# Hash sums in half as many matmuls, late causal masks on VectorE and 64-bit weights scaled in place, in a fused attention kernel

## The chip, the cores and the metric

The kernel runs on one NeuronCore of one Trainium2 chip, and no other core takes part. The metric is the time of one execution of the whole program on the device, in microseconds (us). A core has five engines that run side by side, each through its own list of instructions in order: TensorE (PE in the profile, with its weight loads as PEld), VectorE (DVE), ScalarE (ACT), GpSimd (POOL) and SyncE (SP), which here only starts DMAs. PSUM is the memory that TensorE writes into; SBUF is the working memory. GpSimd has work on SBUF tiles only.

## The reference, cut to what matters

Three layers follow each other, on B = 2 sequences of S = 768 rows and 8 heads of 64 columns. The first is attention between rows with the same hash of 6 bits, the second a causal attention of 4 experts with a choice of 2, the third a feed-forward layer with a gate.

```python
def _attn_ref(q, k, v, proj):                      # q, k, v: 2 x 8 x 768 x 64; proj: 64 x 6
    q_bits = (np.einsum('bhsd,dk->bhsk', q, proj) > 0).astype(np.int64)
    k_bits = (np.einsum('bhsd,dk->bhsk', k, proj) > 0).astype(np.int64)
    powers = 2 ** np.arange(n_bits)
    q_bucket = np.sum(q_bits * powers, axis=-1)
    k_bucket = np.sum(k_bits * powers, axis=-1)
    mask = q_bucket[:, :, :, None] == k_bucket[:, :, None, :]
    scores = np.where(mask, scale * np.matmul(q, k.transpose(0, 1, 3, 2)), -1000000000.0)
    attn = softmax(scores)
    return np.matmul(attn, v)
...
def _moe_ref(x, w_gate, wq, wk, wv, wo):           # x: 2 x 768 x 512
    ...
    for e in range(E):                             # E = 4 experts, heads of 64 columns
        q, k, v = x @ wq[e], x @ wk[e], x @ wv[e]
        causal = np.triu(np.ones((S, S), dtype=bool), 1)
        scores = np.where(causal, -1000000000.0, scale * (q @ k.transpose(0, 2, 1)))
        ye = softmax(scores) @ v @ wo[e]
        out += (the weight of e where e is among the two highest) * ye
    return out
...
def _moe2_ref(x, mu_k, mu_r, w_k, w_v, w_r):       # w_k, w_v, w_r arrive as 64-bit floats
    x_prev = (x moved down by one row)
    xk, xr = mu_k * x + (1.0 - mu_k) * x_prev, mu_r * x + (1.0 - mu_r) * x_prev
    k = np.maximum(xk @ w_k, 0.0)
    return 1.0 / (1.0 + np.exp(-(xr @ w_r))) * (k * k @ w_v)
```

`softmax` and the words in brackets stand for lines that are left out.

## The kernel before

The rows are cut into 12 tiles of 128 (`NU`), tiles 0 to 5 of the first sequence and 6 to 11 of the second. For each tile `i` four groups of steps are recorded: the query (`query_steps`), the hash attention (`lsh_steps`, one score per head, then one product with the values per head), the expert attention (`moe_steps`) and the feed-forward layer (`mix_steps`). Keys come in groups of four heads (`key_steps(b, g)`, four groups in all), weights in `weight_steps`. Almost every operand is kept as a high and a low 16-bit part, so that a product takes three matmuls.

Four things of it matter here.

**The hash.** A query tile is turned by TensorE into `x2`, a key group into `y2`, and `hash_signs` multiplies each turned block of 128 rows with the projection, which stands in `prhl` as a high and a low part of 6 columns each. The two products are added in PSUM by accumulation, so a block takes two matmuls of 6 columns: 16 matmuls for a query tile (8 heads), 48 for a key group (24 blocks). `mark` then compares the sums in `z` (in PSUM) with zero, twice, and writes a large number or zero into spare columns of `nbq` (queries) or `nbk` (keys); these are turned in their place into `x1` and `y1`, and so the score of two rows with different hashes falls far below. `naq` and `nak` are the tiles that hold the high and low parts of a query tile and of half a key group before they are turned.

**The causal mask.** `score(c)` of `moe_steps` handles a pair of experts: TensorE writes both scores (`se`) into PSUM, and then adds `causal`, a triangle of very large negative numbers, to the last 128 columns of each by one more matmul with the identity. The minimum over a row, the exponential and the split into high and low parts (`P_m`, `PHL_m`) follow on VectorE, ScalarE and GpSimd, then a transpose by DMA (`PT_m`). The scores of both attentions share two PSUM buffers (`ps_s`).

**The 64-bit weights.** `split_d` loads the two 32-bit words of each number (`raw`). GpSimd scales the upper words into a tile of their own (`mag`, `wm` in the profile), and VectorE puts the number together from `mag`, `raw` and an exponent that ScalarE made. There are 20 such blocks.

**The order.** Nothing is scheduled while the kernel is built: all operations are recorded, and `arrange` (line 184) puts them into the order of a packed table, `ORDER`; a second table, `HOMES`, gives each tile its buffer. `issue` (line 199) then sends them to the engines, which is why every instruction bears the number of one line, 201. An engine works through its own instructions in that order, whatever it waits for.

Of the kernel before, what the change touches and what calls it, by code (L numbers as in the profile page):

```python
# [17 lines left out]
OP = mybir.AluOpType  # L18
# [210 lines left out]
def tile_lsh_moe_mix(  # L229
# [98 lines left out]
    def turn(dst, src, nm, by_dma=False):  # L328

        if by_dma:  # L330
            nc.sync.dma_start_transpose(dst, src)
            return
        n = src.shape[1] // P
        hn = n // 2
        if n > 8:
            pt = [dps(f"tr_{nm}_{j}").bitcast(F16)[:, :hn * P] for j in range(2)]
        else:
            pt = dps(f"tr_{nm}").bitcast(F16)
            pt = [pt[:, j * hn * P:(j + 1) * hn * P] for j in range(2)]
# [42 lines left out]
    def split_d(src, dst, sc, nm):  # L382
# [3 lines left out]
        mag = sp.tile([P, n], F32, tag="b2", bufs=NB2, name=f"wm_{nm}")  # L386
# [3 lines left out]
        nc.gpsimd.tensor_scalar(mag, top.bitcast(F32), REBIAS, 1.0, op0=OP.mult, op1=OP.mult)  # L390
# [3 lines left out]
        nc.vector.scalar_tensor_tensor(u, mag.bitcast(U32), 3, u, op0=OP.logical_shift_left, op1=OP.bitwise_or)  # L394
# [49 lines left out]
    def key_steps(b, g):  # L444
# [11 lines left out]
        def half(j):  # L456
            if j == 0:
# [40 lines left out]
    def query_steps(i):  # L498
# [4 lines left out]
        def prep():  # L503
# [9 lines left out]
            turn(x2, na.rearrange("p h c -> p (h c)"), f"x2_{i}", i in QD)  # L513

        def hash_():
# [4 lines left out]
            turn(x1, nb.rearrange("p h c -> p (h c)"), f"x1_{i}", i in QD)  # L520
# [19 lines left out]
    def hi_engine():  # L540
        NS[0] += 1
        return "p" if (NS[0] - 1) % 8 < 2 else "a"
# [98 lines left out]
    def moe_steps(i, LAG):  # L641
# [67 lines left out]
        def score(c):  # L709
# [196 lines left out]
c-jq?gAyQ062MwB-LtlB+qP}nwr$(CZQHhO<Jo)n4XIQ@0Km`^+CwHN2&Eu12sp?B(LmuOwt}881NuV;=m)K#7ZifhkPUJ`VJHL9Atw}r;!pxgLUyPKl^_O`  # L906
hYFAjVnbXg2eAObLslpXWuXYn1cS;DAP&TXJdhhAK~;zXRUk4{gX+)>T0nlN1vMZl)P|Zc3uZ$Bh!1&T4xGY#kPs5XX>1JX;V+H|F<}6-fws^QIzeY>2fd*<
=Er)F2ogXlD1fQqJf6i8SRV>v3doAt@Em5xlu!}}!d$q3^WbkD1QDP*CW9nU2n%Bo971VeB20oVFa!p}P}mI(peu}o95@+rVp1rDrLhLqfx0jSE@E8Fjh8Vw
oWV<Y1+QUq7zVj;4@`x4m>kPvUMz}vFazv`wU7cE!cf`=DKS1K!0VU~YvO)Lg$H07^nvwI3!6Y%7!GBy8;pX4m<ZQFYD|N}DL<FRL(t9bmW=QVHiCojD_+G7
PyshWMQjSgC><uo23QXtVOl&4wQ&<9!6VQeDq$V$0V7~K{D$eVG9HCUloab@20R9lDH%RSAxBZ@IQ)(oF%!;*Wl#m{VpZ%5nK3FA;B+vGM$io$O;6C%2`GpE  # L910
U@;s?o8czj!hbOfE{ABe0HV`qc#11vAuNL1xDx)u#jpyV;d4~FgLiQ??2(r^hQ`tdY>16;9KFJcv<4<oW2}bbsR=g43G@+{z*6{x_wWHW!?W}U{=oa#9E}1!
#MjsYx6<D@7Pi0zh(SP~aT|QWH`oeWVjFCY5$FZ}iCdu{Z=>z7op!)EYL9JkC%naza1p*D(qH%v-(x%61?Q;)E}?H2hbGe{_>Mbh3dN<La0teurSvln$Dvr5
nTm2BybS&E3iQRJ6qAUGa526>-Q5U04a2Y>UWH?H4PsG8EaAt&7&rxm_&6=2GZ2xA^IVEgXQ2z0<f*iicF}dXNCR*=jfasq3I}309E9Dm2hPFRRD$PG0y+ot
sVA1=)zlSN&`O#{rMVZLhtYTs5>gp1%X=viC8ojH8!yofn1E|&BA%d|&<Rh{TI!6Ga2+k6eUzM%(KzhD<8cg*#iW#kZoz(<jJIJoU8Vz+f~Me9yaOHiA0EN~
# [90 lines left out]
```

## Time and profile before

| What | us |
|---|---|
| Median of 3 runs (lowest, highest) | 470.1 (467.38, 470.42) |
| The profiled execution, whole | 470.66 |
| Its span, from the first to the last instruction | 468.9 |
| TensorE busy in it | 428.9 |
| VectorE busy | 345.3 |
| ScalarE busy | 345.0 |
| GpSimd busy | 324.2 |
| DMA queue of SyncE, share of 16 DMA engines | 85.4% |

All rows of the profile come from the one profiled execution; its span and the whole time differ by what lies before the first and after the last instruction. An engine that is busy is not always an engine that is waited for: which one sets the pace differs between the first 140 us and the rest, so the profile has to be read by stretches of time. The granted clock of TensorE was 0.981 of full speed on average.

### The profile page before, as it was taken

To read this page: it belongs to the slowest core of one execution; us is meant where nothing else is said; L and a number is where in the kernel's file an instruction comes from. 1 tells how busy PE (TensorE), PEld (TensorE's weight loads), DVE (VectorE), ACT (ScalarE), POOL (GpSimd) and SP (SyncE) were. 2 spreads that over 40 slices of the span, in tenths; PEclk is the share of its full clock that TensorE was granted. 3 is DMA by queue.
4 is the path that set the end of the run, shared out by engine and by line. 5 is a ranking of instruction groups with operands and counts; after the bars stand their busy time and mean duration, and the time that the engine had idled before them with its cause. 6 is when DMAs were issued, how large, how long until landed. Compare 5 with 4: busy or idle time off the path is not lost.

```text
span 468.9 us, 15555 instructions
## 1 busy us (share of the span) xinstructions
PE 428.9 (91%) x6296; PEld 328.6 (70%) x6296; DVE 345.3 (74%) x970; ACT 345.0 (74%) x654; POOL 324.2 (69%) x321
## 2 busy tenths in 40 slices
PE   2965679899899999998999999999999999999996
PEld 1843467677777779787777778687668769867572
DVE  3999989989999779899695667955768644643421
ACT  4369889979999889777985977878777975543320
POOL 5579899879886977876989468857766945362000
PEclk9997889989999999999999999999999999999999
DMA  8978989899999999989999799978998894555101
GB/s 228 284 191 194 198 191 180 171 225 170 181 219 199 204 178 192 191 157 181 164 184 170 158 148 150 179 148 141 141 156 119 140 187 82 126 81 125 46 24 45
DMA packets 227160, 75.59 MB, mean 161 GB/s; under 512 B 218512, under 2 KB 222736, under 8 KB 227088
## 3 DMA queue, kind: packets, MB, share of 16 engines
q1 hardware_dynamic: 225584, 74.48, 85.4%
q8 instruction: 49, 0.80, 0.7%
q10 hardware_dynamic: 1504, 0.11, 0.2%
q14 instruction: 23, 0.19, 0.1%
HBM read 22.14 MB, written 3.15 MB: 54 GB/s over the span
## 4 chain that ended last, share of the span: by engine, by line
PE 61%; DVE 11%; POOL 10%; DMA 8%; issue 6%; ACT 4%; SPq 0%; POOLq 0%; DVEq 0%; ACTq 0%
PE v L201 12%; PE h L201 11%; PE x L201 7%; PE s L201 7%; POOL PHL L201 6%; PE r L201 5%; PE qk L201 5%; DVE P L201 3%; DMA PT<-PHL 3%; PE se L201 3%; PE y L201 3%; PE o L201 3%; PE tr_y L201 2%; PE vg L201 2%; DMA PT_m<-PHL_m 1%
## 5 line engine op out<-in xcount | busy, mean ns | idle before, releaser
L201 POOL TENSOR_TENSOR PHL<-P,PHL 128x768 f16<-128x768 f32 x96 | 159.7, 1672 | 36.1 <-ACT PHL L201 34.4
L201 DVE TENSOR_SCALAR_CACHE_REDUCE P<-s 128x768 f32<-128x768 f32 x96 | 91.0, 951 | 19.1 <-PE s L201 12.7
L201 ACT ACTIVATE P<-P,mx 128x768 f32<-128x768 f32 x96 | 89.1, 928 | 16.3 <-DVE mx L201 15.7
L201 PE MATMUL s<-y,x 128*128 128x384 f16 x384 | 80.7, 336 | 8.7 <-DVE P L201 6.1
L201 PE MATMUL h<-mk,WK 128*128 128x128 f16 x1152 | 72.6, 219 | 0.0
L201 PEld LDWEIGHTS <-WK 128*128 128x128 f16 x1152 | 67.0, 98 | 4.0
L201 PE MATMUL x<-v,PT 128*128 128x64 f16 x1728 | 64.3, 195 | 2.1 <-DVE v L201 2.0
L201 PEld LDWEIGHTS <-PT 128*128 128x128 f16 x1728 | 60.2, 99 | 6.8 <-issue 2.4
L201 ACT ACTIVATE PHL<-P 128x768 f16<-128x768 f32 x72 | 59.9, 839 | 4.9 <-DMA PT<-PHL 1.6
L201 PEld LDWEIGHTS <-x 128*128 128x128 f16 x576 | 40.8, 99 | 28.8 <-issue 10.1
L201 PE MATMUL v<-WV,k2h 128*128 128x512 f16 x192 | 57.1, 379 | 0.0
L201 POOL TENSOR_TENSOR PHL_m<-P_m,PHL_m 128x512 f16<-128x512 f32 (+2 forms) x24 | 34.3, 1429 | 18.6 <-ACT PHL_m L201 10.2
L201 PE MATMUL qk<-xT,WQK 128*128 128x128 f16 x576 | 35.8, 219 | 1.0 <-DVE xT L201 0.5
L201 PE MATMUL v<-WV,k2l 128*128 128x512 f16 x96 | 36.4, 379 | 0.0
L201 PEld LDWEIGHTS <-WQK 128*128 128x128 f16 x576 | 33.1, 98 | 2.6 <-DMA xT<-hl_x 0.9
L201 PE MATMUL r<-WR,mr 128*128 128x512 f16 x144 | 34.5, 379 | 0.0
L201 DVE SCALAR_TENSOR_TENSOR h<-h,t 128x512 f32<-128x512 f32 x24 | 16.6, 694 | 20.7 <-ACT t L201 20.7
L201 ACT ACTIVATE t<-h 128x512 f32<-128x512 f32 x24 | 14.2, 590 | 23.4 <-PE h L201 23.3
L201 DVE TENSOR_SCALAR_CACHE_REDUCE P_m<-se 128x512 f32<-128x512 f32 (+2 forms) x24 | 19.6, 818 | 13.4 <-PE se L201 3.8
L201 PEld LDWEIGHTS <-k2h 128*128 128x128 f16 x192 | 17.0, 98 | 13.2 <-issue 0.2
L201 POOL TENSOR_SCALAR PHL<-P 128x768 f16<-128x768 f32 x24 | 21.0, 876 | 7.5 <-ACT P L201 3.5
L201 ACT ACTIVATE P_m<-P_m,bias_m 128x512 f32<-128x512 f32 (+2 forms) x24 | 19.7, 821 | 7.8 <-DVE P_m L201 7.7
(143 smaller groups left out, 867.8 us busy)
## 6 DMA issues: line engine op xcount, KB each, us to landing
raw_k<-in_moe_w_k_dram SPq DMA_DIRECT2D x8, 512.0 KB, 4.5
raw_v<-in_moe_w_v_dram SPq DMA_DIRECT2D x8, 512.0 KB, 4.3
q<-in_q_dram SPq DMA_DIRECT2D x12, 256.0 KB, 5.3
k<-in_k_dram SPq DMA_DIRECT2D x8, 384.0 KB, 5.2
v<-in_v_dram SPq DMA_DIRECT2D x8, 384.0 KB, 4.7
out_dram<-e SPq DMA_DIRECT2D x12, 256.0 KB, 2.6
raw_r<-in_moe_w_r_dram SPq DMA_DIRECT2D x4, 512.0 KB, 4.5
PT<-PHL SPq DMA_TRANSPOSE x88, 4.3
```

What stands on the lines that cost most here:

```text
L201: getattr(getattr(self.nc, engine), method)(*[real(a) for a in args], **{k: real(a) for k, a in kw.items()})
```

## The change

Four things are changed in the code, and with them both tables.

- `hash_signs` multiplies each block once with all 12 columns of `prhl`. ScalarE copies the 6 low sums of each block from PSUM into a new SBUF tile `zs`, VectorE adds the 6 high sums to them, and `mark` reads `zs` in SBUF where it read `z` in PSUM. 384 hash matmuls become 192; 16 copies on ScalarE and 16 additions on VectorE are new (12 of 48 columns, 4 of 144).
- For tiles 6 to 11 (`MV`) the causal mask is added to the scores by VectorE, in PSUM: one instruction for both experts where a score has at most 512 columns (tiles 6 to 9), else one for each. 24 matmuls of 128 columns go; 16 VectorE instructions come (8 of 256 columns, 8 of 128).
- `split_d` scales the upper words where they are, in `raw`, and `mag` is gone: 20 GpSimd instructions write every second word of `raw` where they wrote a dense tile, and VectorE reads them there.
- `turn` can leave a copy to ScalarE (`engs`), but `KE` and `QE` are empty, so it never does; `HP` is the old rule under a name.

```diff
+KE, QE = {}, {}
+MV = (6, 7, 8, 9, 10, 11)
...
-        z = dps(f"z_{nm}", [P, n, NB])
+        z = dps(f"z_{nm}", [P, n, 2 * NB])
         for j in range(n):
-            for a in (1, 0):
-                nc.tensor.matmul(z[:, j], rows(j), prhl[:, a], start=(a == 1), stop=(a == 0))
-        return z
+            nc.tensor.matmul(z[:, j], rows(j), prhl.rearrange("p a b -> p (a b)"), start=True, stop=True)
+        zs = sp.tile([P, n, NB], F32, tag="b2", bufs=NB2, name=f"zs_{nm}")
+        nc.scalar.activation(zs, z[:, :, NB:], AF.Copy)
+        nc.vector.tensor_tensor(zs, z[:, :, :NB], zs, op=OP.add)
+        return zs
...
-        mag = sp.tile([P, n], F32, tag="b2", bufs=NB2, name=f"wm_{nm}")
         raw = sp.tile([P, n, 2], U32, tag="b4", bufs=NB4, name=f"raw_{nm}")
         LOADS.dma_start(raw.rearrange("p n a -> p (n a)"), src.bitcast(U32))
         top = raw[:, :, 1]
-        nc.gpsimd.tensor_scalar(mag, top.bitcast(F32), REBIAS, 1.0, op0=OP.mult, op1=OP.mult)
+        nc.gpsimd.tensor_scalar(top.bitcast(F32), top.bitcast(F32), REBIAS, 1.0, op0=OP.mult, op1=OP.mult)
...
-        nc.vector.scalar_tensor_tensor(u, mag.bitcast(U32), 3, u, op0=OP.logical_shift_left, op1=OP.bitwise_or)
+        nc.vector.scalar_tensor_tensor(u, top, 3, u, op0=OP.logical_shift_left, op1=OP.bitwise_or)
...
-                                         stop=(a == 2 and j < len(parts) - 1))
+                                         stop=(a == 2 and (i in MV or j < len(parts) - 1)))
             d0 = t0 * P - k0
-            for r in range(2):
-                o = Sv[r] if one else Sv[r][:, j]
-                nc.tensor.matmul(o[:, d0:d0 + P], ident, causal, start=False, stop=True)
+            if i in MV and one:
+                d = both[:, :, d0:d0 + P]
+                nc.vector.tensor_tensor(d, d, causal.unsqueeze(1).to_broadcast([P, 2, P]), op=OP.add)
+            else:
+                for r in range(2):
+                    o = Sv[r] if one else Sv[r][:, j]
+                    if i in MV:
+                        nc.vector.tensor_tensor(o[:, d0:d0 + P], o[:, d0:d0 + P], causal, op=OP.add)
+                    else:
+                        nc.tensor.matmul(o[:, d0:d0 + P], ident, causal, start=False, stop=True)
...
 ORDER = """
-c-jq?gAyQ062MwB-LtlB+qP}nwr$(CZQHhO<Jo)n4XIQ@0Km`^+CwHN2&Eu12sp?B(LmuOwt}881NuV;=m)K#7ZifhkPUJ`VJHL9Atw}r;!pxgLUyPKl^_O`
+c-jru^8*)F7l83|&b{ZHd%oGWv8-h+bGf!`W6QPdWo=o@HkP)yW!rAqeBb}!`Qh^r0JMZQ;2;|mgW^yEvO^9i2j!sxl!4Na2RcJc=mfFA!*`Gu%0gAh1(hK-
...
```

Both tables are new from end to end, and every instruction's number changes. The long run of work is the same: tiles follow each other as before, and most pieces keep their neighbours. Three places show what moved. The first is the start of SyncE's list, which issues the loads (`w32` weights of the expert layer, `q32` and `k32` queries and keys before the split). Before:

```order
L201 DMA w32_qk01_79<-in_moe_wq_dram 128x4x64
L201 DMA q32_0_81<-in_q_dram 128x8x64
L201 DMA k32_0_1_0_83<-in_k_dram 128x2x384
L201 DMA k32_0_1_1_85<-in_k_dram 128x2x384
L201 DMA k32_0_0_1_93<-in_k_dram 128x2x384
L201 DMA k32_0_0_0_95<-in_k_dram 128x2x384
```

Now, on SyncE at the start:

```order
L208 DMA q32_0_81<-in_q_dram 128x8x64
L208 DMA k32_0_1_0_83<-in_k_dram 128x2x384
L208 DMA k32_0_1_1_91<-in_k_dram 128x2x384
L208 DMA w32_qk01_115<-in_moe_wq_dram 128x4x64
L208 DMA k32_0_0_1_117<-in_k_dram 128x2x384
L208 DMA w32_qk01_115<-in_moe_wq_dram 128x4x64
L208 DMA w32_qk00_150<-in_moe_wq_dram 128x4x64
L208 DMA k32_0_0_0_152<-in_k_dram 128x2x384
```

The first query and the first two halves of a key group moved up by one place; the last half of a key group moved down by two.

The second place is the start of VectorE's list, up to the first copies of turned blocks (`tr`) out of PSUM. Before:

```order
L201 CAST prhl_89<-pr32_72 128x6
L201 TENSOR_TENSOR prhl_89<-pr32_72,prhl_89 128x6
L201 SCALAR_TENSOR_TENSOR naq_0_87<-q32_0_81,naq_0_87 128x8x64
L201 SCALAR_TENSOR_TENSOR nak_0_1_0_111<-k32_0_1_0_83,nak_0_1_0_111 128x12x64
L201 SCALAR_TENSOR_TENSOR nak_0_1_1_113<-k32_0_1_1_85,nak_0_1_1_113 128x12x64
L201 COPY x2_0_128<-tr_x2_0_115 128x512
```

Now, on VectorE at the start:

```order
L208 SCALAR_TENSOR_TENSOR nak_0_1_0_85<-k32_0_1_0_83,nak_0_1_0_85 128x12x64
L208 SCALAR_TENSOR_TENSOR naq_0_88<-q32_0_81,naq_0_88 128x8x64
L208 SCALAR_TENSOR_TENSOR nak_0_1_1_93<-k32_0_1_1_91,nak_0_1_1_93 128x12x64
L208 CAST prhl_122<-pr32_72 128x6
L208 COPY y2_0_1_124<-tr_y2_0_1_0_0_103 128x768
L208 COPY x2_0_126<-tr_x2_0_110 128x512
```

The two operations on the projection moved from the head of the list to behind the first three splits.

The third place is VectorE at a late score, that of the first pair of experts of tile 7 (`se_7_0`): the minimum over it (`P_m7_p0`, one instruction per expert) is what stood there before.

```order
L201 TENSOR_SCALAR P_m7_p0_6403,bias_m7_1_6404<-se_7_0_6376 128x256
L201 TENSOR_SCALAR mx_9_5966<-mx_9_5966 128x1
L201 TENSOR_SCALAR P_m7_p0_6403,bias_m7_0_6407<-se_7_0_6376 128x256
L201 SCALAR_TENSOR_TENSOR m32k_6_6343<-o_6_6118,muk_289,x2t_6_1402 128x128
L201 SCALAR_TENSOR_TENSOR m32r_6_6438<-o_6_6118,mur_77,x2t_6_1402 128x128 x2
```

Now, on VectorE at the same score:

```order
L208 TENSOR_TENSOR se_7_0_6210<-se_7_0_6210,consts_74 128x2x128
L208 SCALAR_TENSOR_TENSOR m32r_6_6061<-o_6_5942,mur_78,x2t_6_2244 128x128
L208 TENSOR_SCALAR P_m7_p0_6231,bias_m7_0_6232<-se_7_0_6210 128x256
L208 SCALAR_TENSOR_TENSOR m32k_6_6064<-o_6_5942,muk_318,x2t_6_2244 128x128 x2
L208 TENSOR_SCALAR P_m7_p0_6231,bias_m7_1_6241<-se_7_0_6210 128x256
```

The addition of the mask stands two places ahead of the first minimum, with a piece of the feed-forward layer (`m32r`) between them.

## Rows read from the trace of the kernel before

**Rows 1.** Busy time of each engine in three stretches, granted clock, DMA share.
```profile
core 0: us, PE busy (x) PEld busy (x) DVE busy (x) ACT busy (x) POOL busy (x), PEclk, DMA share, GB/s
...
20.00:68.00 48.00, 31.77 (x404) 23.30 (x402) 45.71 (x107) 39.02 (x70) 41.52 (x37) 0.86 0.84 198
68.00:140.00 72.00, 65.27 (x1061) 52.28 (x1059) 68.03 (x208) 66.80 (x142) 64.22 (x69) 0.97 0.97 193
140.00:440.00 300.00, 296.62 (x4515) 229.75 (x4514) 211.68 (x618) 227.91 (x428) 206.35 (x197) 1.00 0.91 155
```

**Rows 2.** TensorE's costliest wait from 140 us on: total us, times, longest.
```profile
PE y L201 <- DMA PT_m<-PHL_m: 1.7, 2, 1.4
```

**Rows 3.** The chain that ended last, its last piece on an engine: start, us, what.
```profile
465.09 0.69 DVE e L201
```

**Rows 4.** Instructions of TensorE in order of time (start, us, count), 188 to 201 us.
```profile
188.98 1.34 PE L201 MATMUL z_k<-prhl,y 128*128 128x6 f16 x48
190.18 0.69 PE L201 MATMUL x<-v,PT 128*128 128x64 f16 x18
190.70 0.60 PE L201 MATMUL v<-WV,k2h 128*128 128x512 f16 x2
...
200.49 0.29 PE L201 MATMUL se<-consts 128*128 128x128 bf16 x2
200.61 1.34 PE L201 MATMUL z_k<-prhl,y 128*128 128x6 f16 x48
```

**Rows 5.** The start in order of time: two DMA issues, ScalarE, GpSimd, VectorE.
```profile
1.22 0.50 SPq L201 DMA_DIRECT2D q<-in_q_dram  x1
1.77 2.61 SPq L201 DMA_DIRECT2D k<-in_k_dram  x4
...
6.82 0.84 ACT L201 ACTIVATE nak<-k 128x768 f16<-128x768 f32 x1 [0.43 <-DMA k<-in_k_dram]
6.98 0.62 POOL L201 MEMSET nbk<- 128x624 f16 x1
7.07 0.55 DVE L201 CAST prhl<-pr 128x6 f16<-128x6 f32 x1 [7.07 <-DMA pr<-in_proj_dram]
7.91 2.71 POOL L201 TENSOR_SCALAR nbk<-k 128x768 f16<-128x768 f32 x2 [0.32 <-DMA k<-in_k_dram]
8.35 3.07 DVE L201 SCALAR_TENSOR_TENSOR nak<-k,nak 128x768 f16<-128x768 f32 x2
13.41 0.94 DVE L201 SCALAR_TENSOR_TENSOR nak<-k,nak 128x768 f16<-128x768 f32 x1
```

**Rows 6.** Groups, shapes apart: count, busy us, mean ns, idle before and its releaser.
```profile
L201 DVE TENSOR_SCALAR nbk<-z_k 128x72 f16<-128x72 f32 x16 | 2.9, 223 | 0.6 <-PE z_k L201 0.6
L201 DVE TENSOR_TENSOR y<-y,rse 128x256 f32<-128x256 f32 x12 | 5.0, 419 | 1.1 <-PE y L201 1.0
L201 DVE SCALAR_TENSOR_TENSOR m32k<-o,muk,x2t 128x128 f32<-128x128 f32 x48 | 15.6, 344 | 0.6 <-POOL mr L201 0.4
L201 POOL TENSOR_SCALAR wm_k<-raw_k 128x512 f32<-128x512 f32 x8 | 6.0, 756 | 3.6 <-DMA raw_k<-in_moe_w_k_dram 3.5
L201 ACT ACT_TABLE_LOAD x16 | 20.5, 1283 | 3.4 <-issue 3.1
L201 DVE SCALAR_TENSOR_TENSOR naq<-q,naq 128x512 f16<-128x512 f32 x12 | 11.0, 920 | 0.0
```

**Rows 7.** Tiles z_q and naq: ns (shortest/median/longest), first and last start.
```profile
L201 DVE TENSOR_SCALAR nbq<-z_q x24: 192/200/211, 16.5 to 322.9; 128x48 f16<-128x48 f32 x24
L201 DVE SCALAR_TENSOR_TENSOR naq<-q,naq x12: 679/741/1522, 7.7 to 260.4; 128x512 f16<-128x512 f32 x12
```

**Rows 8.** All engines in order of time, 294 to 300 us, three instructions of it.
```profile
294.61 3.25 POOL L201 TENSOR_TENSOR PHL<-P,PHL 128x768 f16<-128x768 f32 x2 [0.73 <-ACT PHL L201]
296.33 2.08 DVE L201 TENSOR_TENSOR hl_x<-x,hl_x 128x512 f16<-128x512 f32 x1 [0.36 <-ACT hl_x L201]
...
299.21 0.82 PE L201 MATMUL s<-y,x 128*128 128x384 f16 x4 [1.00 <-DVE P_m_p L201]
```

More of the change, by code (lines that the diff above doesn't have):

```diff
@@ L37, with HP @@
 OKV = 61440.0
+def HP(n):
+    return n % 8 < 2
+KE, QE = {}, {}
+MV = (6, 7, 8, 9, 10, 11)
 QD, KD, XD, YD = (8, 9, 10, 11), (), (8, 9, 10, 11), (8, 9, 10, 11)
@@ L541, in hi_engine @@
         NS[0] += 1
-        return "p" if (NS[0] - 1) % 8 < 2 else "a"
+        return "p" if HP(NS[0] - 1) else "a"
     def softmax(Sv, n, scale, sm, bias, nm, masked=None, by_pe=None):
@@ L910 @@
[L910 to L914, printed above, removed]
@@ new lines @@
+D`OVSir?Tjup0*QXc$f-Xb((-?D!W{$HLeH{)T-}A6G*rSOp`g4-A6__yhKY+n5H^;TlMfYhgcp!aJA)KVu6R4r%cKe2+D-AvVHMG=}2RXu6BPQal<<7qKzU
+fj^)o&V`(q3)ewzTns;AEj$RBVIGX5zR(ZGQ!`u-UobvRp!qP7E}<u;=6D(NU=?hNQ7IZNfGJc4?_mO30tsmZB%-f)A0OaUx`IGgaVboq$s}|Qm5`cXbc#VS
+sW!gAN4N}H;Bt70kMR|*fR=b2x6%n}g*Wguw#NVP3H}P=H$Y-K4iE7r-oke1XcN4_h42(NLM)0+-?_Iq6UV{{c!t|(Gi-rHaFW_!du)r-s1v53t<V9tQ%Bqe
+o$(}0r&Dl>0v!UP=eUGE;5+<?QOIZvB&V{jyc>e=aR>cLhoKehq|>yND!66z8%1b14#kvI&Ygx-l!WF{U+jm!U>96Y|G>X+2GozhVR#mP!k@9C8-Rx>DaE04
+&>cr&4;+O@U_MoH{qZQQpsv^x2V!M+n5wvc=oloUJ(QZ#P#HG}SJHX73Zt<XR(0KQFa1krC@l@f?_D)_maf4CI6~tf9bJS4)EjHK>aGuFq)e2a&e0|Ki^k)1
@@ new lines @@
+xB(MzBHn}yw3>d!u{aLL;O}%9{-zn!-35OICSg=R8P`w`mzi!sR+@rGX*|rNRdkGY(POv+-_TU7=^}otTS$v2nqNyjT@;^%dbxG9&)<e=_&d&_Su`Dg!+rDz
+?Wegk&dtDCxSozvHu{z>P%XECW>a?R?Fv$DSI6a~TvUi!xJ$H~HqvD}K#OS(&c)d{4|7u<%1i%2VQT5dyL{BjEyTt62j-ypxQRAXep-ZAXbaVKMW~N6-{1Y>
+o<LuBp6a_2)X-g|gR}sj!ZWxF_n@_F;M%wXRL|Xqt5ljEz;l@3iqb>4MlWEZTZt=h8AkWlDTZ(4O41FA=^MKN?h(ZDvHeXN=9c3R?nf8T$MNxfTtD1Rb?sez
+`~bzMI8AbsT@zP|zN4mY6@G#x*w*d$AEBA+;O^3G>gVpzElS`=xX-W#zd#vUjb*96ti_S;E8L?8G|&Mq#d?$g+qp-S5C^&Y^pFzz%GA+4p=b1*UQlyaj$XoJ
+dP<$#D3=JU&>Q;A{pu3qOZtyqQF$um5BURrutOZ;I=j*C6?AcguPF)s?%vZ|O5{J#JNigps45-yN%1S8JLoG=C8|hWT{Rl&{_)l66OD1*+-vyPm-cVqh@auU
@@ new lines @@
+^WPIWa5d;H9P`e-gMi+#`%GE=Pwr>;jju_yDY>8G()pwQJvhwfJ(lr_{YhVoj{7<^-A!{T{3(CJr}T{3{W`qlXS!J~hZjuZ)B6nmvR9n#>QX9i7;zbWCO^lm
+#|>D>Z^Ym>qdIfq>QhrH>>E%N*My?F<`m5p@mG99`hl9!kF*J6;EGUObNZydtdH-K`OH3oS$uB41-D{!w+(mUX}=ryU}_)3#l&*Hyien|;|^>=Eh!4-@li1v
+#&myTbj<5_Vk~#Y58|sn7N+&N{57A?Kl6L>FO1^~`q(b6tKcj8zp<8&jd3t8#>2Bdzc1<=Q6*p5SMhcHbN|B6bqm})H{X@?`*1&g@2~s8T);P`V!o;`?uW}u
+oxtDvKionW&s}iU{9?Dro%84YFdo9|-A;D^hjId!&<*DlE~QKEwz`-8mA~Li`0D<(f8&?9ByNMN>;HC%-Ex=6rE)d=Hn-jFa4X#^x7xL#z^$mJZ%ZS1glu&C
++zPkf9dK*hF1ObG=|=J<x7(G_rLMNG=SQ(|gj>^1f6KR{Wo|Slb@hEG>P%gzD>d*x_=9e<+v4`Pb#AZw%azn4u7$ttTl@ADg`;u@>PRhp8$XfT`e;0v+xhnX
@@ new lines @@
+u>02mKk$wGA@`4K=zr&n{)UgvW4M){#K_&~s5|C5_~WjlpTWQKIBx7uxT*Z3f9LP`yM88*W#aKXjZeBJ{*;@;Z+%Rj%hS23|BWB|NB>XJ^Er3Mopo{ewEOCN
+P&41$zxN;f&vf3+<I;MC@A)Zw-!pge!l${jzv!;G`TW@5a+ll<chy~XH{D17$uHoAyokHgPxPOk#ZUZI?n%Aqsqf-%yWVt-m-0yILw%_qDfg#e=r+gZoBY{-
+@dIce4Wh2Tn}4NeI4<Ae#ry}~;<KF0&F1cYW$58ky9<1Y2h&Bq%*%KM_wlhf9uJ`<yqs4u$aVhATN&jBpW~nW&;C4*lDmA5`}%?YK0o9K{D>bjNes^5(z~bJ
+&-e6${1+bV@3{W{8OP^z?j^tCUA&v0^MCB*1@GY}97leYRXkea${2|!d-*S3&BJ_Jw~o`eUcR^YvYuJSN_@HIGP-R%#1Hkq_yPWJP9O<o9}o8lI3d60{rrYS
+ruyqHlT%s4BYhM}#B2F2Z{T;lku$rflEo$CBs@+=_@q2uHgO^evYAKu13cOv<Y@AhCrETj$?rL<`^IH+M>sJjXOkVgg=0ue`M|McJ0Im#oZY47V?4&E;E9rs
@@ L962 @@
+TE;kW42V8N!5i0O|L93mg2}yh)+<oc$@{9E`P>?p2eJ6hy`Dbjfw@ewNl>IX)`(aJfzag-jmMbe_Tc|T7DP{y#apZvG}_15K73#0He%<4$E$LlHNV4mtw<J)
+<{)uh1>@>c&zWN9{#fy@wC*li)NK<+(_5NM%z187yxor*p37-w8-4=K+#E~
 """
```

95 lines of the change are left out of this document (41 added, 54 removed).

## The prediction, made before the changed kernel ran

> **What bounds the kernel now.** The averages of the whole run say that TensorE is busiest, but they mix two kinds of stretch, so I began with the busy times by stretch [rows 1]. From 20 to 68 us VectorE is busy 45.71 of 48 us and TensorE only 31.77: there VectorE sets the pace, with GpSimd (41.52) and ScalarE (39.02) behind it. From 68 to 140 us four engines are near full, none alone at the limit (VectorE 68.03, ScalarE 66.80, TensorE 65.27 of 72). From 140 to 440 us TensorE is busy 296.62 of 300 us and VectorE only 211.68. The waits of TensorE behind 140 us bear it out: the costliest, for a DMA that brings the turned weights of the expert attention, is 1.7 us in all [rows 2]. The chain of what ended last closes with VectorE's last result at 465.09 us [rows 3], and this end is the same in both kernels. So a microsecond taken from TensorE behind 140 us is worth nearly a microsecond, and one added to VectorE there nothing; before 68 us it is the other way round. The change takes from TensorE and gives to VectorE in both. The sum is made against the profiled execution, 470.66 us, which lies 0.56 above the median of the runs.
>
> **TensorE behind 140 us.** In the row of time order 48 hash matmuls of 6 columns start at 188.98 and the next work at 190.18 [rows 4]: 1.20 us, 25 ns each. The product with 64 columns takes 29 ns (18 from 190.18 to 190.70), so the number of columns hardly shows, and I cost a matmul of 12 columns at 25 ns too. Key groups of the second batch: 2 x 24 fewer x 25 ns = 1.2 us. Queries 6 to 11: 6 x 8 x 25 ns = 1.2 us. A pair of mask matmuls takes 0.12 us (200.49 to 200.61) [rows 4], 12 pairs are gone: 1.4 us. Together 3.8 us. Queries 3 to 5, in the mixed stretch, are 3 x 8 x 25 ns = 0.6 us, of which I count half, since TensorE is one of four near the limit there. Sum **-4.1 us**. Were 12 columns to cost 29 ns, the 96 matmuls that are left behind 140 us would take back 0.4.
>
> **The start.** VectorE does nothing until the projection arrives at 7.07 us. Then a cast of 6 elements takes 0.55 us and ends at 7.62, just when GpSimd's fill of `nbk` (6.98 + 0.62) ends [rows 5]: it looks held back by it. Two `nak` beside GpSimd's work on `nbk` (7.91, 2.71 long) take 3.07 us, one alone at 13.41 takes 0.94 [rows 5]: some 0.6 us lost on each. Now the first `nak` heads VectorE's list. Its keys are issued one place earlier, 0.55 us (1.77 less 1.22), so ScalarE's half, ended at 7.66 before (6.82 + 0.84), may end at 7.11: VectorE starts when it did, but without the blocked cast, 0.5 us. If the two `nak` also go free, 1.7 us are won; if GpSimd holds the first one for one more fill of 0.62 instead, 0.5 is lost. I take **-1.0 us**, the cast and one of the two `nak`, with bounds of -1.7 and +0.5.
>
> **The additions to the hash sums, until 68 us.** VectorE adds two key groups (144 elements) and three queries (48). The trace has no such form; the nearest rows are a comparison of 72 elements at 223 ns and a tensor operation of 256 at 419 ns [rows 6], which puts 144 at 0.30 us, and the mark of 48 elements at 200 ns [rows 7]. 2 x 0.30 + 3 x 0.20 = 1.2 us; instructions in a row overlap somewhat, I take 0.9: **+0.9 us**. ScalarE copies the low sums ahead of them; its 9 idle us of 48 cover five copies, each surely shorter than the 0.84 us of a `nak` half [rows 5]. If not covered, they delay VectorE by at most the 1.5 us that five of 0.30 make.
>
> **The marks.** This is the term with the widest bounds. A mark now reads SBUF where it read PSUM. From PSUM it was never held: shortest 192, median 200, longest 211 ns over 24 [rows 7]. An operation of VectorE that reads SBUF alone can be: `naq` takes 679 ns at its shortest and 1522 at its longest [rows 7], 920 in the mean [rows 6], so it loses 0.24 us on average, with GpSimd busy for much of the time. And near 296 us one `hl_x` took 2.08 us beside GpSimd's `PHL`, after which TensorE stood still for 1.00 us [rows 8]. Until 68 us there are 14 marks, 8 of key halves and 6 of queries, in 7 pairs; the bounds are nothing and 14 x 0.6 (the loss of a `nak` above) = 8.4 us. I take one average loss for each pair, since a mark is far shorter than `naq` and can slip in between two of GpSimd's instructions: 7 x 0.24 = **+1.7 us**. The Trainium skill says in "SBUF — State Buffer", section "Who interferes with whom", that VectorE and GpSimd share a pair of SBUF ports as an exclusive lock, held for a whole instruction, that single-source operations between SBUF tiles in a two-port mode contend for it, and that with a source in PSUM they can't enter that mode. By that rule every mark is moved from the forms that never wait into those that may, and the sum would come out as in the second rival below; the row of `naq` agrees that waiting occurs, no row shows it of a mark.
>
> **68 to 140 us.** Three additions (0.6) and three pairs of marks (3 x 0.24 = 0.7) for queries 3 to 5, half of it on the path in a stretch where VectorE is busy 94%: **+0.7 us**.
>
> **Edits at nothing.** The late masks on VectorE: 8 of 256 elements by 0.42 and 8 of 128 by 0.34 [rows 6] are 6.1 us, hidden in the 88 us that VectorE is idle from 140 to 440 (300 less 211.68); without that cover 6.1, the third rival. The scaling in place: 20 operations of 756 ns [rows 6], which read every second word before and now write so as well; VectorE reads `raw` in such steps already. At 0; were the eight early ones to double, 6 us on GpSimd, which has 6.5 idle us from 20 to 68. Two more loads of ScalarE's tables, by the order, at 1.28 us [rows 6]: covered by 72 idle us behind 140. That the new order makes or removes waits otherwise, I can't price beyond the 1.7 of [rows 2].
>
> **The sum.** -4.1 - 1.0 + 0.9 + 1.7 + 0.7 = -1.8: 468.9 against the profiled 470.66, and **468.3 us** against the median.
>
> **Rivals.** First, the marks aren't held (a pair that slips in, as every mark from PSUM does) and the start gives its full 1.7: -1.8 - 2.4 - 0.7 = -4.9; with half the wait of 1.7 gone in the new order, 0.8, it is -5.7, **464.4 us**. For it: marks are short. Against it: GpSimd is busy 87% of the time there.
>
> Second, on the other side, every mark is held for 0.6 us: the 1.7 becomes 8.4 until 68 us, and the 0.7 of the mixed stretch becomes half of 0.6 + 6 x 0.6, 2.1; -4.1 - 1.0 + 0.9 + 8.4 + 2.1 = +6.3, **476.4 us**. It decides from 0.23 us a mark: with 17 marks that count (14 and half of 6), 17 x 0.23 = 3.9 is what the other terms (-4.1 - 1.0 + 0.9 + 0.3) win. For it: the `nak` at the start; against it: the median of `naq`, 741 ns, is only 62 above its shortest, so most go nearly free.
>
> Third, the mask on VectorE is a new wait: it stands between a score and its minimum, on one of the two PSUM buffers that all scores share, so the next score on TensorE can start only when VectorE got to both. If VectorE comes late each time, 6.1 us land on TensorE: -1.8 + 6.1 = +4.3, **474.4 us**. For it: TensorE did wait 1.00 us for a minimum [rows 8]; against it, it did so only there, in 300 us.
>
> Last, a matmul of 12 columns may cost twice one of 6, so that only the masks are saved: 1.4 instead of 4.1, and 471.0 us; I hold that as part of the forecast's own case, since 64 columns at 29 ns speak against it.
>
> **Chances.** The forecast's case, 466.5 to 471.0 us, has 0.42; the free marks 0.33; the held marks 0.15; the late mask 0.10. A measurement of this kernel can tell about 1% from no change, 465.4 and 474.8 us. Faster than that are some seven tenths of the first rival (0.23) and a little of the forecast's case (0.05): 0.28. Slower are three quarters of the held marks and half of the late masks: 0.17. The rest, 0.55, is the same. The range goes from 463.0, the first rival with all of the 1.7 us wait gone (463.5) and a little more, to 474.5, which takes in the late mask and leaves out the upper half of the held marks.
>
> **What would show it.** Right: 192 hash matmuls at 25 ns a piece; VectorE at work on `nak` by 7.2 us; the first 68 us of work shorter or longer by no more than 2 us; marks of `zs` with a median near 200 ns and some above 500; TensorE's waits behind 140 us still near 3 us. The second rival: marks over 500 ns throughout, and idle TensorE before 68 us that grows. The third: waits of TensorE's scores for VectorE's minimum or mask behind 140 us, several us in all. I would be wrong altogether if the granted clock, 0.86 of full speed from 20 to 68 us [rows 1] (the levels are 1.2 and 2.4 GHz), fell for longer because TensorE has less to do early, or if the new order made a wait that no row here shows.

## The result, and the profile after

The changed kernel takes 472.12 us (median of 16 runs, 470.72 to 474.25), the kernel before 467.44 us in the 16 runs now beside it (464.08 to 470.75): ratio 1.0106, 95% interval 1.0085 to 1.0128. It is slower by 4.7 us, where 1.8 us less was forecast, and its absolute time lies within the range only because the three runs of before that were shown (470.1) lay high. Its profiled execution has a span of 471.3 us.

The busy times by stretch, in the columns of [rows 1]:

```profile
20.00:68.00 48.00, 33.54 (x376) 23.43 (x377) 47.63 (x110) 40.36 (x75) 39.72 (x37) 0.83 0.84 189
68.00:140.00 72.00, 60.77 (x990) 48.66 (x987) 71.38 (x205) 63.64 (x136) 61.93 (x69) 0.98 0.93 193
140.00:440.00 300.00, 294.42 (x4392) 225.64 (x4390) 226.70 (x645) 233.52 (x442) 207.79 (x198) 1.00 0.89 154
```

VectorE is now busy almost without a pause from 20 to 140 us (47.63 of 48, 71.38 of 72, where it had 45.71 and 68.03; the time for which an instruction is held up counts as busy), and TensorE, ScalarE and GpSimd all do less from 68 to 140 us than before. So the start and the middle are paced by VectorE more than they were.

The groups of VectorE's new and changed instructions (count, busy us, mean ns, idle before):

```profile
L208 DVE TENSOR_SCALAR nbq<-zs_q 128x48 f16<-128x48 f32 x24 | 19.3, 816 | 0.1
...
L208 DVE TENSOR_SCALAR nbk<-zs_k 128x72 f16<-128x72 f32 x16 | 5.7, 393 | 0.0
...
L208 DVE TENSOR_TENSOR se<-se,consts 128x256 f32<-128x256 f32 x8 | 3.4, 422 | 2.5 <-PE se L208 2.5
...
L208 DVE TENSOR_TENSOR se<-se,consts 128x128 f32<-128x128 f32 x8 | 2.3, 293 | 2.2 <-PE se L208 2.2
L208 DVE TENSOR_TENSOR zs_q<-z_q,zs_q 128x48 f32<-128x48 f32 x12 | 2.4, 199 | 0.0
...
L208 DVE TENSOR_TENSOR zs_k<-z_k,zs_k 128x144 f32<-128x144 f32 x4 | 1.2, 297 | 0.0
```

The additions and the masks cost what was forecast (0.20 and 0.30 us; 0.42, and 0.29 for 0.34). The marks do not: a query mark took 0.20 us and takes 0.82 in the mean, a key mark went from 223 to 393 ns in the mean [rows 6, 7] (the median key mark takes 194 ns; a few long ones make the mean). Two stretches in order of time show why, first around 37 us and then around 114 us, with the rows of GpSimd, VectorE and TensorE:

```profile
36.65 1.64 POOL L208 TENSOR_TENSOR PHL<-P,PHL 128x768 f16<-128x768 f32 x1
36.76 1.57 DVE L208 TENSOR_SCALAR nbq<-zs_q 128x48 f16<-128x48 f32 x1
...
38.26 1.42 POOL L208 TENSOR_SCALAR w_qk<-w_qk 128x512 f32<-128x512 f32 x1
...
39.12 0.60 DVE L208 TENSOR_SCALAR nbq<-zs_q 128x48 f16<-128x48 f32 x1
...
39.78 0.50 PE L208 MATMUL tr_x<-consts,nbq 128*128 128x128 f16 x3 [3.12 <-DVE nbq L208]
...
112.95 3.24 POOL L208 TENSOR_TENSOR PHL<-P,PHL 128x768 f16<-128x768 f32 x2
...
114.24 2.00 DVE L208 TENSOR_SCALAR nbq<-zs_q 128x48 f16<-128x48 f32 x2
...
116.30 0.62 PE L208 MATMUL tr_x<-consts,nbq 128*128 128x128 f16 x8 [1.29 <-DVE nbq L208]
```

Each of these marks of 48 elements begins while an instruction of GpSimd runs and ends just after that ends; it is held, as the text calls it from here on: 36.76 + 1.57 = 38.33 against 36.65 + 1.64 = 38.29, 39.12 + 0.60 = 39.72 against 38.26 + 1.42 = 39.68. At 114.24 the pair of marks takes 2.00 us: the first waits for the end of one `PHL`, the second for the end of the next. Over the whole trace 22 of the 40 marks take more than 0.3 us, and each of the 22 ends 0.04 or 0.05 us after an instruction of GpSimd. TensorE, which has to turn the marked tile, waited 3.12 and 1.29 us at these two places. From 20 to 140 us its waits for `nbq` are 5.4 us in three places, where they were 2.1 in one.

The start went a little better than forecast; VectorE in order of time:

```profile
7.32 0.96 DVE L208 SCALAR_TENSOR_TENSOR nak<-k,nak 128x768 f16<-128x768 f32 x1 [7.32 <-ACT nak L208]
...
8.79 0.95 DVE L208 SCALAR_TENSOR_TENSOR nak<-k,nak 128x768 f16<-128x768 f32 x1
...
9.66 0.17 DVE L208 CAST prhl<-pr 128x6 f16<-128x6 f32 x1
```

The first `nak` starts at 7.32 and both take 0.96 or less, where two took 3.07 [rows 5]; the cast takes 0.17 for 0.55. The first hash of keys starts on TensorE at 13.27 us, where it started at 15.66.

### The profile page after: what moved, and what is told of

The parts are those of the page before. It is cut to its first block, busy times and chain, and to the rows that moved or that the text cites. A ratio compares the mean times of both kernels' runs of the same rounds, so it can differ in the third digit from the quotient of the medians.

```text
span 471.3 us, 15157 instructions
## 1 busy us (share of the span) xinstructions
PE 425.9 (90%) x6080; PEld 321.5 (68%) x6080; DVE 366.5 (78%) x1002; ACT 350.4 (74%) x672; POOL 321.4 (68%) x321
## 4 chain that ended last, share of the span: by engine, by line
PE 39%; DVE 6%; DMA 4%; issue 3%; ACT 3%; POOL 2%; SPq 1%; DVEq 0%; ACTq 0%; POOLq 0%
PE v L208 10%; PE h L208 8%; PE r L208 4%; PE s L208 4%; DMA PT<-PHL 3%; PE x L208 3%; PE qk L208 2%; PE y L208 2%; PE se L208 2%; POOL PHL L208 2%; PE o L208 2%; DVE P L208 2%; PE vg L208 1%; DMA xT<-hl_x 1%; PE tr_y L208 1%
## 5 line engine op out<-in xcount | busy, mean ns | idle before, releaser
L208 POOL TENSOR_TENSOR PHL<-P,PHL 128x768 f16<-128x768 f32 x96 | 159.6, 1673 | 30.6 <-ACT PHL L208 24.8
L208 PEld LDWEIGHTS <-x 128*128 128x128 f16 x480 | 38.2, 99 | 30.5 <-issue 8.8
L208 PE MATMUL qk<-xT,WQK 128*128 128x128 f16 x576 | 38.8, 224 | 1.7 <-DVE xT L208 1.1
L208 PEld LDWEIGHTS <-WQK 128*128 128x128 f16 x576 | 35.1, 100 | 4.7 <-issue 1.6
L208 PE MATMUL r<-WR,mr 128*128 128x512 f16 x144 | 35.7, 379 | 0.0
L208 POOL TENSOR_TENSOR mk<-m32k,mk 128x512 f16<-128x512 f32 x12 | 14.4, 1198 | 20.7 <-ACT mk L208 20.6
```

The source lines that it names most:

```text
L208: getattr(getattr(self.nc, engine), method)(*[real(a) for a in args], **{k: real(a) for k, a in kw.items()})
```

## The experiments

**The marks read PSUM again** (`marks_psum`). The marks follow the addition directly, since the table's later places would keep the PSUM buffer too long.

```diff
-        nc.vector.tensor_tensor(zs, z[:, :, :NB], zs, op=OP.add)
-        return zs
+        nc.vector.tensor_tensor(z[:, :, :NB], z[:, :, :NB], zs, op=OP.add)
...
+        return z[:, :, :NB]
```

> Changed kernel, with one thing undone: the addition writes the sums back into the hash tile in PSUM, and the two marks that follow it read them there, right behind the addition (in the table's places for them nothing is issued). Same instructions in number and size. Theory (marks that read SBUF are held by GpSimd): the marks fall from a mean of 816 and 393 ns to about 200 and 223 ns, 17.7 us of VectorE's time in all, of which 9.6 lie before 140 us where VectorE sets the pace; the time falls from 472.1 to 462.5 to 466.5 us, ratio to the kernel before 0.990 to 0.998. Rival (the new order costs the time): 471 to 472 us, ratio 1.007 to 1.010.

Measured: 464.88 us, ratio 0.9962 (0.9937 to 0.9987). Marks 202 and 224 ns. With this undone the change is a gain: the loss is the marks'. The run changes the source of the marks and also their place; the two are told apart by `packed` below, where the marks keep their place.

**Is it the order?** (`old_hash_masks_pe`): the arithmetic of before, except for the scaling, in the order of the changed kernel. The copies, the additions and VectorE's masks are recorded, but not issued; the marks stand where the addition stood.

```diff
+            for a in (1, 0):
+                nc.tensor.matmul(z[:, j, :NB], rows(j), prhl[:, a], start=(a == 1), stop=(a == 0))
...
+            for r in range(2):
+                o = Sv[r] if one else Sv[r][:, j]
+                nc.tensor.matmul(o[:, d0:d0 + P], ident, causal, start=False, stop=True)
```

> The code of before in the order of the changed kernel: hash by two accumulated matmuls of 6 columns, marks read PSUM (issued where the addition stood), late masks on TensorE; no copy, no addition. Only the scaling in place and both tables are as changed. Shows what the order alone does. Theory (the order by itself is worth nothing or a little): 466 to 468.5 us, ratio 0.997 to 1.002. Rival (the new order is the loss): 471 us or more, ratio from 1.007.

Measured: 466.05 us, ratio 0.9984 (0.9959 to 1.0009). The order by itself (with the scaling in place) does nothing that can be told from none, though the interval leaves room for a gain of almost 2 us; the rival falls.

**The SBUF source alone, in the old order** (`before_marks_sbuf`), and its control (`before_copies_only`), in which the last line reads `return z`.

```diff
+        if n != H:
+            return z
+        zs = sp.tile([P, n, NB], F32, tag="zs", bufs=1, own=True, name=f"zs_{nm}")
...
+        nc.vector.tensor_copy(zs, z)
...
+        return zs
```

The tile `zs` of 192 bytes a row has a buffer of its own (`own`), and each copy stands directly behind its matmuls.

> Kernel before, in its own order, with one thing added: VectorE copies the 48 sums of each query tile from PSUM into an SBUF tile right behind the matmuls, and the query marks read them there (key marks stay as they were). Theory (an SBUF source lets GpSimd hold a mark): the query marks rise from 201 ns to 600 to 900 in the mean; 12 of the 24 lie before 140 us and lose 0.4 to 0.7 us each, 5 to 8 us; with the copies, 470 to 475 us, ratio 1.006 to 1.017. Rival (the marks of the changed kernel were slow by what stands beside them in its order): marks under 300 ns, no slower than the next kernel.

> The kernel of the line above as a control: the 12 copies are made, but the query marks read PSUM as in the kernel before. 12 copies of 0.2 us on VectorE, 6 of them before 140 us: 467.2 + 1 us or less, ratio 0.999 to 1.004, marks at 200 ns. Its distance from the kernel above is the price of the SBUF source alone: 4 to 8 us by the theory, under 1 us by the rival.

Measured: 477.97 us, ratio 1.0214 (1.0179 to 1.0250), and for the control 470.54 us, ratio 1.0065 (1.0039 to 1.0091). The groups of the first, then of the control:

```profile
L211 DVE TENSOR_SCALAR nbq<-zs_q 128x48 f16<-128x48 f32 x24 | 13.9, 599 | 0.1
```

```profile
L211 DVE TENSOR_SCALAR nbq<-z_q 128x48 f16<-128x48 f32 x24 | 4.4, 200 | 0.0
...
L211 DVE COPY zs_q<-z_q 128x48 f32<-128x48 f32 x12 | 2.4, 204 | 6.8 <-PE z_q L211 6.8
```

The source alone costs 7.4 us in an order that has nothing else of the change. With the copies the time went beyond the 470 to 475 us that I expected, and the marks, at 599 ns, came to the lower end of theirs. The control was dearer than expected (2.8 us instead of 1): the copies stand right behind the matmuls, and VectorE was idle for 6.8 us ahead of them, waiting for TensorE.

**Which form is held?** Four kernels change only the shape in which a mark walks its elements. `odd_marks` leaves out the first block of each, and so some of the work (one head in eight has no hash); `threes` and `twos` walk all of them with 3 or 2 groups of columns outermost; `packed` keeps the query sums in that order of threes in SBUF, so that a query mark reads one run and writes 3 groups.

```diff
+        nc.vector.tensor_scalar(dst[:, 1:, :NB], z[:, 1:], 0.0, OKV, op0=one, op1=OP.mult)
...
```

```diff
+        nc.vector.tensor_scalar(dst[:, :, :NB].rearrange("p n (c b) -> p c n b", c=3),
+                                z.rearrange("p n (c b) -> p c n b", c=3), 0.0, OKV, op0=one, op1=OP.mult)
...
```

```diff
+        zt = sp.tile([P, n * NB], F32, tag="b2", bufs=NB2, name=f"zs_{nm}")
+        zs = zt.rearrange("p (c n b) -> p n c b", c=3, b=2)
...
+        zh, zl = (z[:, :, a * NB:a * NB + NB].rearrange("p n (c b) -> p n c b", c=3) for a in (0, 1))
+        nc.scalar.activation(zs, zl, AF.Copy)
+        nc.vector.tensor_tensor(zs, zh, zs, op=OP.add)
+        return zt.rearrange("p (c n b) -> p c n b", c=3, b=2)
...
```

> Changed kernel, but every mark leaves out the first block of rows: 7 of 8 heads of a query, 11 of 12 blocks of a key half; the spare columns are filled with zeros instead (GpSimd's fills grow from 52 to 64 columns a block), so one head in eight has no hash. The marks still read SBUF. Theory A (the hold needs a form that VectorE can split into two equal halves, as the Trainium skill's VectorE page would have it): marks of an odd count near 200 ns, 464 to 467 us, ratio 0.993 to 1.000. Theory B (any read of SBUF by VectorE alone is held): marks at 400 to 800 ns, 471 to 473 us, ratio 1.007 to 1.013.

> Changed kernel, every mark whole and from SBUF, but walked in another order: the 6 columns of a block as 3 groups of 2, the groups outermost (3 x 8 x 2 for a query, 3 x 12 x 2 for a key half), so that the outermost count is odd while the elements are all there, 48 and 72. Theory (a mark is held only in a form that can be split into two equal halves): marks near 200 and 223 ns, shortest and longest within 30 ns, 464 to 466 us, ratio 0.992 to 0.998, as with the marks that left out a block. Rival (the odd number of blocks, or the work that was left out, made that run fast): marks at 400 to 800 ns, 471 to 473 us, ratio 1.007 to 1.013.

> Control for the line above: the same reordered walk with 2 groups of 3 outermost (2 x 8 x 3, 2 x 12 x 3), an even count. Theory: held as in the changed kernel, marks of 400 to 850 ns in the mean, 471 to 473 us, ratio 1.007 to 1.013. Rival (any reordered walk escapes): 464 to 466 us.

> Changed kernel, with the sums of a query tile kept in SBUF in the order 3 x 8 x 2 (groups of two columns outermost): ScalarE and VectorE write them so, and the two marks read them as one run of 48 and write 3 x 8 x 2. Nothing is left out; the key marks stay as changed. Theory (a mark is held where the outermost counts of source and target are both even or equal: 48 and 8, 3 and 3, 2 and 2 were held, 42 and 7, 66 and 11 were free): 48 against 3 is free, query marks 175 to 215 ns, key marks about 390 in the mean as before; 464 to 467 us, ratio 0.993 to 0.999. Rival (the marks that left out a block were free for their smaller size, or since they began inside the tile): query marks of 700 to 850 ns, 471 to 473 us.

Measured, with the query marks' ns (shortest/median/longest) as the view of their tile gives them:

| Kernel | Source, target of a query mark | ns | us | ratio (interval) |
|---|---|---|---|---|
| changed | 48, 8 x 6 | 176/636/1682 | 472.12 | 1.0106 (1.0085 to 1.0128) |
| `odd_marks` | 42, 7 x 6 | 181/188/197 | 464.39 | 0.9914 (0.9883 to 0.9944) |
| `threes` | 3 x 8 x 2, 3 x 8 x 2 | 171/608/1680 | 472.16 | 1.0093 (1.0059 to 1.0127) |
| `twos` | 2 x 8 x 3, 2 x 8 x 3 | 197/632/1705 | 471.51 | 1.0093 (1.0062 to 1.0125) |
| `packed` | 48, 3 x 8 x 2 | 184/194/204 | 463.79 | 0.9930 (0.9906 to 0.9954) |

The outermost count is the number of groups in the slowest-moving step of a walk: 8 in 8 x 6, 3 in 3 x 8 x 2. My expectation for `threes` was wrong: an odd outermost count on both sides is held like an even one. What is free is an even source against an odd target (42 and 7, 48 and 3; the key marks of `odd_marks`, 66 and 11, took 205 to 222 ns). In `packed`, whose key marks are as changed, these are still held. The same place as at 114 us above, first in `odd_marks` and then in `packed`:

```profile
109.23 3.25 POOL L208 TENSOR_TENSOR PHL<-P,PHL 128x768 f16<-128x768 f32 x2
...
110.52 0.29 DVE L208 TENSOR_SCALAR nbq<-zs_q 128x42 f16<-128x42 f32 x2
```

```profile
111.26 3.26 POOL L208 TENSOR_TENSOR PHL<-P,PHL 128x768 f16<-128x768 f32 x2
...
112.54 0.30 DVE L208 TENSOR_SCALAR nbq<-zs_q 128x48 f16<-128x48 f32 x2
```

Both pairs run through in 0.3 us beside a `PHL` that made the pair of the changed kernel take 2.00. These forms agree with a rule of the Trainium skill, "VectorE: DVE Perf Modes", section "Mode 2×_2P — use both read ports for one tensor": the two-port mode wants source and target in SBUF, not in PSUM, and outermost counts that are even on both sides, or odd and equal. My expectations for `odd_marks` and `threes` had left out the case of odd and equal counts. That a source without gaps counts as one run of 48 is inferred from them (42 against 7 x 6 would be 7 against 7 otherwise), and not shown in another way.

**The price of the two gains.** The late masks went back to TensorE (as in the diff of `old_hash_masks_pe`) in the changed kernel and in `marks_psum`, `threes` and `packed`. Two matmuls for a block, into separate columns, were put back in three.

```diff
+            for a in (0, 1):
+                nc.tensor.matmul(z[:, j, a * NB:a * NB + NB], rows(j), prhl[:, a], start=True, stop=True)
```

> Changed kernel, with the masks of tiles 6 to 11 added by TensorE again (24 matmuls of 128 columns; the 16 additions on VectorE are not issued, all else stands where it stood). Theory (the masks on VectorE lie beside TensorE's work and cost nothing): 12 pairs of 0.12 us come back on TensorE, 473.5 us, ratio 1.012 to 1.015. Rival (the mask on VectorE holds up scores or delays the marks' neighbours): the time falls, to 466 to 470 us.

> Changed kernel with the sums added and read in PSUM, and the late masks on TensorE again. Against the run with only the marks undone (464.9 us) it prices the masks where no mark is held: 12 pairs of 0.12 us, 466.3 us, ratio 0.998 to 1.002; if the masks on VectorE cost something of their own there, it is 465 or less. Against the run with the whole old hash and old masks (466.0 us) it prices the halved matmuls: 2.4 us behind 140 us less the additions would make it 464 to 465; equal times would say that the halved matmuls return no more than the additions cost.

> The kernel with 3 groups outermost, and the late masks on TensorE again. By the working of the prediction 12 pairs of 0.12 us come back: 1.4 us more than with 3 groups and the masks on VectorE. If the mask on VectorE costs as much as it saves, which the runs with sums in PSUM (464.9 and 464.7 us) suggest, the two are equal within 1 us: 464 to 466 us.

> The kernel above with the late masks on TensorE again. By the working of the prediction 1.4 us more than the kernel above; by the earlier pairs of runs (473.5 against 472.1, 464.7 against 464.9, 471.8 against 472.2) between 0.4 less and 1.4 more. Within 1 us of the kernel above would say that the masks on VectorE return about nothing.

> Changed kernel, but each block of the hash is multiplied twice with 6 columns, into the two halves of the same 12 sums; everything else as changed. Prices the halved matmuls: 192 more, of 25 ns each, 96 of them behind 140 us (2.4 us), 24 between 68 and 140 us (0.6), 72 before, where TensorE waits anyway. Theory: 472.1 + 2.4 to 3.0 = 474.5 to 475.1 us, ratio 1.015 to 1.017. Rival (the halved matmuls gain nothing, since a matmul's cost is hidden or 12 columns cost two of 6): 472.1 us, ratio 1.010.

> The kernel with 3 groups outermost, and two hash matmuls of 6 columns for each block again (into the two halves of the 12 sums). Prices the halved matmuls where no mark is held, as TensorE is then waited for in all but the first stretch: 96 x 25 ns behind 140 us and 24 before, 2.4 to 3.0 us more than with one matmul: 466.5 to 468.5 us. Rival (they return nothing, as the earlier run with two matmuls, +0.5 us, could be read): equal within 0.5 us.

> The packed kernel with two hash matmuls of 6 columns for each block again. With the query marks free, TensorE is waited for behind 140 us: 96 x 25 ns = 2.4 us there, up to 0.6 between 68 and 140: 2.4 to 3.0 us more than the packed kernel. Rival (the halved matmuls return little, as in the two earlier pairs, +0.5 us each): 0 to 1 us more.

| Base | us | masks on TensorE | two matmuls |
|---|---|---|---|
| changed | 472.12 | 473.47 (ratio 1.0133, 1.0099 to 1.0166) | 472.66 (1.0119, 1.0083 to 1.0155) |
| `marks_psum` | 464.88 | 464.73 (0.9934, 0.9909 to 0.9959) | |
| `threes` | 472.16 | 471.83 (1.0090, 1.0054 to 1.0125) | 472.69 (1.0110, 1.0075 to 1.0144) |
| `packed` | 463.79 | 464.57 (0.9954, 0.9929 to 0.9978) | 466.45 (0.9991, 0.9971 to 1.0011) |

With the query marks free, the second matmuls cost 2.7 us, as forecast for them, uncertain by 1.2 us by the spread of the runs. Where marks are held they cost 0.5, twice, each uncertain by 1.0 us or more and expected at 2.4 to 3.0; that can't be told from nothing. That VectorE is then waited for in their place is argued, not shown. A pair in which no mark is held agrees: `marks_psum_masks_pe` lies 1.3 us below `old_hash_masks_pe` (2.3 if each is set against the runs of before beside it), where my expectation had the halved matmuls less the additions at 1 to 2. The masks gave 1.4, -0.2, -0.3 and 0.8 us, each uncertain by 0.7 to 1.4 us: their worth is not settled; the mean of the four, 0.4, is less than the forecast's 1.4. The price of a matmul itself is plain; the hash of the last key group in order of time, in `packed` and in `packed_two_matmuls`:

```profile
200.16 0.75 PE L208 MATMUL z_k<-prhl,y 128*128 128x12 f16 x24
200.77 0.69 PE L208 MATMUL x<-v,PT 128*128 128x64 f16 x18
```

```profile
198.64 1.34 PE L208 MATMUL z_k<-prhl,y 128*128 128x6 f16 x48
199.84 0.68 PE L208 MATMUL x<-v,PT 128*128 128x64 f16 x18
```

24 of 12 columns take 0.61 us, 48 of 6 take 1.20: 25 ns each, with 6 columns and with 12.

## Why the prediction was wrong

**The step that failed** is the marks: "I take one average loss for each pair, since a mark is far shorter than `naq` and can slip in between two of GpSimd's instructions". It put +1.7 us on the path until 68 us and about 0.4 (half of 0.7) from there to 140. The runs show 8.3 us for the query marks alone (472.12 of the changed kernel less 463.79 of `packed`), and 7.4 us for the same in the old order. A short instruction does not slip in: none of the 30 marks of the changed kernel that began more than 0.03 us into an instruction of GpSimd ended before that did, and with `PHL` the wait went up to 1.65 us. So what is lost is set by GpSimd's instruction and not by the mark's own length, and both marks of a pair can lose. In the changed kernel's trace the marks lose 4.9 us until 68 us (queries 3.3, keys 1.5) and 4.6 from there to 140, against their means of before.

The rows of `naq` [rows 7] could have told this; their mean and median were read wrongly. The median of 741 ns is the middle between two kinds: six of the 12 take 679 to 693 ns, six take 789 to 1522. In the kernel before, one of each kind:

```profile
45.28 1.20 POOL L201 TENSOR_SCALAR nbq<-q 128x512 f16<-128x512 f32 x1
45.93 1.09 DVE L201 SCALAR_TENSOR_TENSOR naq<-q,naq 128x512 f16<-128x512 f32 x1
...
149.08 1.16 POOL L201 TENSOR_TENSOR mr<-m32r,mr 128x512 f16<-128x512 f32 x1
150.35 0.68 DVE L201 SCALAR_TENSOR_TENSOR naq<-q,naq 128x512 f16<-128x512 f32 x1
```

The first begins while GpSimd works and ends 0.54 us after it, the second begins when GpSimd is done. All six long ones end 0.54 or 0.55 us after an instruction of GpSimd, and the four that lie between 20 and 100 us are all of this kind: there the loss was 0.11 to 0.81 us apiece. So "most go nearly free" does not hold for the stretch that the forecast priced, and the average of 0.24 mixes in the six beside which no instruction of GpSimd had been running for more than 0.02 us when they began.

**What came instead** is the second rival, which had 0.15. Its price of 0.6 us a mark is what query marks lost in the mean (816 less 201 ns), while key marks lost 0.17; it decides from 0.23 us a mark, and at +6.3 us it came nearer to the measured +4.7 than the forecast. That its sum came so near is partly luck: it had 8.4 us until 68 us, where the marks lost 4.9, and nothing behind 140 us, where the next point finds some 2. The rule of the Trainium skill set beside the marks ("SBUF — State Buffer", section "Who interferes with whom") spoke against this change, and the trace agrees: held marks end 0.04 or 0.05 us after GpSimd's instruction.

**A second, smaller error** is that a microsecond added to VectorE behind 140 us costs nothing; that was read off its idle share there, which is an average. The changed kernel's chain of what ended last runs through late query marks (start, us, what):

```profile
225.81 0.57 DVE nbq L208
226.45 0.51 DVE nbq L208
...
333.58 0.43 DVE nbq L208
334.97 1.58 DVE nbq L208
```

These are 3.1 us; in `packed` the marks on the chain behind 200 us come to 0.45. From the start of the last key hash to the end of the span it is 471.3 - 204.19 = 267.1 us in the changed kernel and 464.8 - 200.16 = 264.6 in `packed`, 2.5 less. The start of the first is this row:

```profile
204.19 0.75 PE L208 MATMUL z_k<-prhl,y 128*128 128x12 f16 x24
```

Each is a single execution, but two more such pairs agree: 2.1 us with the masks on TensorE (`late_masks_on_pe`, `packed_masks_pe`) and 1.4 with two matmuls (`two_hash_matmuls`, `packed_two_matmuls`). So held marks took back 1.4 to 2.5 us where TensorE sets the pace, though the waits of TensorE that name `nbq` there are only 0.2 us: on the chain the delay reaches it through VectorE's work behind the marks. In the kernel before the same stretch is 468.9 - 200.61 = 268.3 us [rows 4], but with the arithmetic of before in the new order (`old_hash_masks_pe`) 266.3, so the distance from before to `packed` can't be put down to the hash and the masks alone.

**What was right.** The halved matmuls: -2.7 forecast, 2.7 measured with free query marks. The additions: 0.20 and 0.30 us. The start: `nak` at 7.32, and both free where the forecast counted on one; its worth was not measured by itself. The order: nothing that shows, 0.9984. The scaling in place: GpSimd's eight early ones took 721 ns in the mean for 756, on the path nothing. The first rival, free marks, gave 464.4 us; `packed` and `marks_psum` came to 463.8 and 464.9, though from a kernel before that lies 2.7 us lower than the forecast's, so that they gained 2 to 3 us and not 5.7. (Its sum takes off the whole 0.7 of the mixed stretch, of which about 0.3 are additions that stay.) Summed with measured sizes where there are any: matmuls -2.7, masks -0.4, query marks +8.3, and the additions +0.9 and the start -1.0 as forecast: +5.1, against 4.7. The key marks' share, 16 x 0.17 = 2.7 us of VectorE, was not measured by itself.

The granted clock does not account for it: from 0 to 20 us it was 0.89 in the changed kernel and 1.00 before, but also 1.00 in `marks_psum` and 0.87 in `marks_psum_masks_pe`, which take the same time. From 20 to 68 us it was 0.83 for 0.86 before, and 0.73 in `threes`, which takes no longer than the changed kernel. Over all runs its mean was 0.981 both in `twos` (471.5 us) and in `packed` (463.8).

The version that beats both is `packed`, 0.9930 of the kernel before: the change as it is, with the query sums kept in SBUF in another order.

## What to carry to other kernels

Before a small VectorE operation is moved from a PSUM source to an SBUF source, look at what GpSimd runs at that place: the price is the rest of GpSimd's instruction, not the size of the operation. Read such a risk one instruction at a time, beside what the other engine does then: a mean or a median over instructions that met GpSimd and others that did not is the price of neither. Where the source has to be in SBUF, a target whose outermost count is odd, against an even run in the source, went free here.

## What the runs showed of the hardware that was not expected

- An SBUF-to-SBUF comparison with one source took 171 to 1705 ns beside GpSimd with even or equal outermost counts, and 181 to 204 ns with an even source and an odd target, with the same kinds of GpSimd instructions beside it. Nothing was lost by the second form: unheld, both take about 0.17 to 0.22 us.
- A two-source operation between SBUF tiles (`naq`) was held too: 6 of 12 in the kernel before, each ending 0.54 or 0.55 us after an instruction of GpSimd.
- GpSimd's `PHL` lost nothing by it: 1672 ns in the mean before and 1673 after.
- The same 192 matmuls less gave 0.5 us twice with held query marks and 2.7 us with free ones, each uncertain by 1.0 to 1.2 us.
